# Attention and gated feed-forward on one core: inner rows left in PSUM, softmax sums of four key tiles folded into one, reciprocals laid out 128x9

## The chip, the cores and the metric

The kernel runs on one NeuronCore of a Trainium2 chip. The metric is the device time of one execution in microseconds (us), the median of several runs. The core has a matrix engine (TensorE, PE in the profile; its weight loads are PEld), a vector engine (VectorE, DVE), an activation engine (ScalarE, ACT), a general engine (GpSimd, POOL) and an engine that issues the DMAs (SyncE, SP). Matmul results land in PSUM, 8 banks of 128x512 fp32; everything else lives in SBUF.

## What is computed

8 batches of 8 heads, 576 positions, head size 64. For each head:

```
scores = q k^T / 8 + min(-(cum_i - cum_j), 0)      # cum: running sum of max(s, 0); masked above the diagonal
attn   = exp(scores - rowmax) / (sum + 1e-9)
x      = attn v                                     # heads side by side: 576 x 512 for each batch
h      = max(x w_in, 0)                             # 576 x 1024
c      = cw0 * h[row - 1] + cw1 * h[row] + cw2 * h[row + 1]
out    = (h * sigmoid(c)) w_out                     # 576 x 512 for each batch
```

## The kernel before

**Attention.** Heads go in 32 pairs `p`. Queries lie along the free axis, keys on partitions, in NT = 5 key tiles of 128 (the last has 64 keys). By causality key tile `t` serves only queries from 128t on: widths W_T = 576, 448, 320, 192, 64. For each pair TensorE computes shift scores (`sh_mm`, L1089), of which VectorE takes row maxima (`sh_max`, L1134, which reads PSUM), then the scores proper (`sc_mm`, L1211). ScalarE turns scores into exponentials (`sc_exp`, L1233) in the SBUF tile `pt`, one for each head of the pair, and GpSimd clears what lies above the diagonal (`sc_mask`, L1246, for pairs from B0 = 8 on).

**Sums.** `sums` (L1289) adds the exponentials over the keys by matmuls with a one-hot 128x32 weight. It cuts the 576 queries into 4 pieces of RS = 144, one for each 32-column strip of the array, so that four such matmuls run beside each other. Head 0 goes to strips 0 to 3, head 1 to strips 3 to 0, so each strip of 32 partitions in one bank (`sb_`) holds one piece of each head in its first two rows. All five key tiles are summed: 28 calls a pair, each of which the trace shows as two matmul instructions. `pv_mm` (L1271) then multiplies the exponentials with `v` into the two banks `pv`, of which there is one set.

**The normalization chain** of a pair: `guard` (ScalarE, L1308) copies the sums' bank, 128x144, to `rs`; `inverse` (VectorE, L1313) takes the reciprocal of all 128x144; `store_ri` (DMA, L1318) writes it to DRAM; `spread` (two DMAs, L1327) reads it back, repeated over 64 partitions for each head; `norm` (VectorE, L1335) multiplies `pv` with it and frees `pv`; `x_hi` and `x_lo` (L1350, L1354) split the result into two fp32r parts.

**Feed-forward** (`moe_h`, `moe_o`). A batch needs the x of its four pairs. It is done in two halves of 288 rows and eight inner tiles `f` of 128, taken two at a time (`fp`). For each f: 12 matmuls of 290 columns into one PSUM bank `hb` (`h_mm`, L1386); `relu` (ScalarE, L1397) from the bank to the SBUF tile `ht`, after which the bank is free; `center` (ScalarE L1409 or VectorE L1411) writes cw1 * h to `ct`; two `tap`s (VectorE, L1422) add the neighbours from `ht`. For two f together: `gate` (ScalarE, L1438, 576 wide), `mul` (VectorE, L1444, 576 wide, ct * ht), and a split into two fp32r parts `u` (L1451, L1455). `moe_o` (L1483) multiplies u with w_out, 24 matmuls for each output tile, and `evac` (L1500) moves it out.

**Order.** Every step is a task; a planner written in the kernel (`Sched.play`) simulates the engines with an estimated cost of each task and fixes the order of each engine at build time. What it takes next is set by due times, the table `DUE`, one number for each task in the order of their creation. Buffers are handed out by the planner from pools: 6 PSUM banks (beside the two of `pv`), 3 `pt`, 3 `ht`, 3 `ct`. A task whose option ends in `True` is not planned beside another such task on the other of VectorE and GpSimd. For pairs from B0 on, TensorE's work on pair n's scores, pair n+1's shift scores and pair n-1's `sum` and `pv` is one uninterrupted burst in the order of `ORDER`: sh0, sum, pv, sh1, sc0, sh2, sc1, sc2, sh3, sc3; it starts when all that its members need is there. Each sh and sc step takes two banks. Between bursts TensorE does feed-forward work. The tiles `ht` and `ct` also serve, early on, to prepare the weights.

Of the kernel before, what the change touches and what calls it, by code (L numbers as in the profile page):

```python
# [11 lines left out]
F32 = mybir.dt.float32  # L12
# [18 lines left out]
B1 = 6  # L31
SCRATCH = 1024
# [1566 lines left out]
```

## Time and profile before

| | |
|---|---|
| median of 3 runs | 806.12 us (805.84 to 806.18) |
| profiled execution | 809.6 us |
| its span, first to last instruction | 807.9 us |
| PE busy | 774.9 us, 96% |
| DVE, ACT, POOL busy | 544.8, 439.5, 328.7 us |

The span is that of one profiled execution; its own time is 1.7 us longer than the span and 3.5 us longer than the median of the runs. Busy times are unions of the engine's instructions, so that four matmuls beside each other count once.

### The profile page before, as it was taken

The numbers are of one execution on the slowest core, as the hardware profiler recorded it, in microseconds if no ns is written. First come the engines' busy times: TensorE is split into PE (matmuls) and PEld (weight loads), VectorE is DVE, ScalarE is ACT, GpSimd is POOL, SyncE is SP. The second block draws the span as 40 slices with busy tenths as digits, with TensorE's granted clock in tenths as the row PEclk, the third lists the DMA queues.
The fourth block names the chain that finished last, engine by engine and source line by source line (L and its number), as shares of the span: only waits on it lengthen the run. The fifth ranks groups of instructions, "written<-read, shape, count | busy, mean of one in ns | idle before, by whom it ended". The sixth has DMA issues, their size and how long they took to land.

```text
span 807.9 us, 21422 instructions
## 1 busy us (share of the span) xinstructions
PE 774.9 (96%) x8557; PEld 690.7 (85%) x8557; DVE 544.8 (67%) x1310; ACT 439.5 (54%) x989; POOL 328.7 (41%) x508
## 2 busy tenths in 40 slices
PE   2899899999999999999999999999999999999998
PEld 1566566898999989998998989998898989998998
DVE  7789979747675867766566757667576576825532
ACT  5355446746455646546555646646554555744543
POOL 7122324344534455544435445553435454422122
PEclk9999989999999999999999999999999999999999
DMA  7654354221423232241414233241414221111001
GB/s 241 209 146 150 109 153 145 86 83 46 141 68 124 77 119 96 79 138 53 141 49 132 87 111 105 75 137 57 140 49 125 96 84 43 43 35 42 17 29 37
DMA packets 57369, 78.77 MB, mean 97 GB/s; under 512 B 6521, under 2 KB 39609, under 8 KB 57209
## 3 DMA queue, kind: packets, MB, share of 16 engines
q1 hardware_dynamic: 57269, 77.40, 30.2%
q8 instruction: 67, 1.10, 0.6%
q14 instruction: 33, 0.27, 0.1%
HBM read 63.94 MB, written 13.19 MB: 95 GB/s over the span
## 4 chain that ended last, share of the span: by engine, by line
PE 90%; DVE 4%; ACT 3%; DMA 1%; issue 1%; POOL 0%; SPq 0%; ACTq 0%; DVEq 0%; POOLq 0%
PE ps L1483 26%; PE ps L1386 25%; PE ps L1211 15%; PE pv L1271 11%; PE ps L1289 7%; PE ps L1089 4%; DVE ps L1134 2%; DMA ek<-bx 1%; PE ps L1101 1%; PE ps L1215 1%; ACT pt L1233 1%; PE ps L1095 1%; PE ps L1160 0%; ACT bx L784 0%; DVE ct L880 0%
## 5 line engine op out<-in xcount | busy, mean ns | idle before, releaser
L1483 PE MATMUL ps<-u,wo 128*128 128x288 f32 x1536 | 220.3, 299 | 0.7 <-ACT ob L1500 0.5
L1386 PE MATMUL ps<-x,wi 128*128 128x290 f32 x1536 | 217.5, 298 | 0.3 <-ACT pt L1233 0.2
L1422 DVE SCALAR_TENSOR_TENSOR ct<-ht,cw_sb,ct 128x288 f32<-128x288 f32 (+1 forms) x256 | 154.6, 617 | 84.7 <-ACT ct L1409 81.2
L1483 PEld LDWEIGHTS ps<-u,wo 128*128 128x128 f32 x1536 | 208.3, 188 | 3.6 <-ACT ob L1500 0.7
L1386 PEld LDWEIGHTS ps<-x,wi 128*128 128x128 f32 x1536 | 209.7, 190 | 1.4 <-ACT pt L1233 0.6
L1233 ACT ACTIVATE pt<-ps,bias_sb 128x288 f32<-128x288 f32 (+4 forms) x384 | 154.3, 478 | 88.7 <-PE ps L1211 88.1
L1455 POOL TENSOR_TENSOR u<-ct,u 128x576 fp32r<-128x576 f32 x64 | 94.2, 1477 | 234.2 <-ACT u L1451 201.0
L1134 DVE CUSTOM_DVE_ANT_0 ps<-ps,bb 128x288 f32<-128x288 f32 (+2 forms) x260 | 108.3, 454 | 60.0 <-PE ps L1089 30.6
L1211 PE MATMUL ps<-s 64*128 64x288 f32 (+4 forms) x1152 | 122.8, 309 | 5.7 <-DVE r L1134 4.2
L1066 POOL TENSOR_SCALAR_AFFINE_SELECT bb<-bb 128x256 f32<-128x256 f32 (+1 forms) x130 | 59.4, 466 | 129.5 <-DVE r L1134 102.3
L1211 PEld LDWEIGHTS ps<-s 64*128 64x128 f32 x1152 | 98.3, 190 | 15.7 <-DVE r L1134 10.0
L1025 POOL TENSOR_TENSOR s<-raw,s 128x1152 fp32r<-128x1152 f32 x31 | 83.2, 2684 | 48.1 <-DVE s L1021 36.8
L1271 PE MATMUL pv<-pt,v 128*32 128x448 f32 (+4 forms) x1536 | 96.6, 395 | 1.0 <-DVE rb L1335 1.0
L1397 ACT ACTIVATE ht<-ps 128x289 f32<-128x289 f32 x128 | 52.7, 411 | 80.0 <-PE ps L1386 79.3
L1271 PEld LDWEIGHTS pv<-pt,v 128*32 128x32 f32 x1536 | 60.0, 111 | 33.0 <-issue 26.2
L1246 POOL TENSOR_SCALAR_AFFINE_SELECT pt<-pt 128x128 f32<-128x128 f32 (+1 forms) x240 | 67.7, 302 | 22.0 <-ACT pt L1233 20.4
L1211 PE MATMUL ps<-eq,ek 64*128 64x288 f32 (+4 forms) x384 | 68.5, 323 | 0.0
L1409 ACT ACTIVATE ct<-ht,cw_sb 128x288 f32<-128x288 f32 x121 | 64.9, 536 | 5.4
L1089 PE MATMUL ps<-s 64*128 64x288 f32 (+4 forms) x384 | 61.9, 345 | 3.7 <-DVE r L1134 1.8
L1289 PE MATMUL ps<-pt,onehot 128*32 128x144 f32 (+4 forms) x1792 | 61.4, 273 | 0.2 <-ACT pt L1233 0.2
L1438 ACT ACTIVATE ct<-ct 128x576 f32<-128x576 f32 x64 | 43.5, 680 | 31.4 <-DVE ct L1422 30.6
L1289 PEld LDWEIGHTS ps<-pt,onehot 128*32 128x32 f32 x1792 | 54.8, 113 | 6.5 <-issue 1.1
(90 smaller groups left out, 671.0 us busy)
## 6 DMA issues: line engine op xcount, KB each, us to landing
raw<-qk SPq DMA_DIRECT2D x32, 576.0 KB
bb<-cum_d SPq DMA_DIRECT2D x26, 576.0 KB
v<-vp SPq DMA_DIRECT2D x32, 320.0 KB
rb<-ri_d SPq DMA_DIRECT2D x64, 144.0 KB
outT<-ob SPq DMA_DIRECT2D x64, 144.0 KB
ht<-w_out SPq DMA_DIRECT2D x16, 256.0 KB
w<-w_in SPq DMA_DIRECT2D x8, 512.0 KB
ri_d<-ri SPq DMA_DIRECT2D x32, 72.0 KB
```

Of the source, the lines that this page charges most:

```text
L1025: tt_on(e)(st[:, 0:2, :], R_t[raw.slot], st[:, 2:4, :].bitcast(F32), op=ALU.subtract)
L1089: nc.tensor.matmul(dst[j], l, S_t[sb.slot][r, 2, c0:c1], start=True, stop=not early)
L1134: nc.vector.tensor_tensor_reduce(out=src, in0=src, in1=in1, scale=1.0, scalar=acc if c0 else -3.0e38, op0=ALU.add, op1=ALU.max, accum_out=acc,
L1211: nc.tensor.matmul(dst[j], l, m, start=(k == 0), stop=(k == 3))
L1233: nc.scalar.activation(PT_t[pts[j].slot][0:jt, O_T[t] + c0 : O_T[t] + c1], bank(pb, o, o + c1 - c0)[0:jt], AF.Sigmoid, bias=bias_sb[0:jt, ...
L1246: nc.gpsimd.affine_select(out=reg, in_=reg, pattern=[[1, dg]], compare_op=ALU.is_ge, fill=0.0, base=0, channel_multiplier=-1,)
L1271: nc.tensor.matmul(pvt[gs, o0 : o0 + c1 - c0], vt[0:jt, t, gs], PT_t[pts[g // 2].slot][0:jt, O_T[t] + c0 : O_T[t] + c1], start=(t == 0), s ...
L1289: nc.tensor.matmul(bank(sb_, o0, o0 + b_ - a_)[32 * g : 32 * g + 32], onehot[:, j, :], src[:, a_ - c0 : b_ - c0], start=t == 0 and j == 0, ...
L1386: nc.tensor.matmul(bank(hb, 0, XW), l, r, start=(k == 0), stop=(k == len(seq) - 1))
L1422: nc.vector.scalar_tensor_tensor(cc[:, lo:hi], h_[:, sh + lo : sh + hi], cw_sb[:, 3 * f + k : 3 * f + k + 1], cc[:, lo:hi], op0=ALU.mult, ...
L1455: tt_on(e)(uu[:, 1], C_t[ct.slot], uu[:, 0].bitcast(F32), op=ALU.subtract)
L1483: nc.tensor.matmul(bank(pb, 0, HS), l, r, start=(fp == 0 and k == 0), stop=(fp == NF // 2 - 1 and k == len(seq) - 1),)
```

## The change

1. **Inner rows stay in PSUM.** `relu` writes its result back over the bank `hb`; `center` (now ScalarE only), both `tap`s and `mul` read the bank. The bank is held until `mul`, not until `relu`. `gate` and `mul` are done for each f (288 wide, 128 of each) and no longer for two (576 wide, 64 of each). `ht` is no longer used by the feed-forward, and `tap` and `mul` lose the flag `True`.
2. **Partial sums of the exponentials**, for pairs from D0 = 7 on (25 of 32). For each head a 128x448 tile, taken from the pool `ht`, gets key tile 0 (queries 128 on) + key tile 1, then + tile 2 (320 wide), then + tile 3 (192 wide), by tensor_tensor adds on VectorE or GpSimd. `sums` then multiplies the one-hot weight with the first 128 queries of tile 0, this partial tile, and tile 4: 12 calls a pair for 28. The new adds are waited for by `sum`, and so by the start of the burst.
3. **Reciprocals 128x9.** A new step `gather` (two DMAs) brings the 2 x 4 rows of 144 sums from `rs` into `rc`, 128x9; `inverse` is taken of that; `store_ri` writes 4.6 KB instead of 74 KB; `spread` reads the same bytes from other places.
4. `DUE` has 3780 numbers for 3470, and all of them are new.

```diff
+D0 = 7
 DUE = (
...
-    ri_t = const.tile([P, RS], F32, name="ri")
+    RW = 2 * S // P
+    rc_t, ri_t = (const.tile([P, RW], F32, name=n) for n in ("rc", "ri"))
-    ri_d = dram.tile([P, RS], F32, name="ri_d")
+    ri_d = dram.tile([P, RW], F32, name="ri_d")
...
+        dense = p >= D0
+        acc = [buf("ht"), buf("ht")] if dense else []
+        added = []
+
+        def partial(j):
+            return H_t[acc[j].slot].rearrange("p a c -> p (a c)")[:, 0 : S - P]
+
+        def key_sum(j, t):
+            def run(e):
+                a = partial(j)
+                src = PT_t[pts[j].slot]
+                o = P * (t - 1)
+                (nc.vector if e == "DVE" else nc.gpsimd).tensor_tensor(
+                    a[:, o:], src[:, P : S] if t == 1 else a[:, o:],
+                    src[:, O_T[t] : O_T[t] + W_T[t]], op=ALU.add,
+                )
+            return run
+
+        if dense:
+            for t in range(1, L):
+                for j in range(2):
+                    t_ad = add(
+                        f"ad{p}.{j}.{t}",
+                        [("DVE", c_tt(W_T[t]), True), ("POOL", c_pool(W_T[t]), True, 2.0)],
+                        [m for k, h, m in masks if h == j and (k == t or t == 1 and k == 0)]
+                        + ([added[-2]] if t > 1 else []),
+                        tq - 4, key_sum(j, t), alloc=[acc[j]] if t == 1 else [],
+                        uses=[pts[j]] + ([acc[j]] if t > 1 else []),
+                    )
+                    added.append(t_ad)
+
+        def sums(e):
+            if dense:
+                todo = [(0, 0), (1, 0), (0, 1), (1, 1), (L, 0), (L, 1)]
+            else:
+                todo = [(t, j) for t in range(NT) for j in range(2)]
+            for t, j in todo:
...
+                c1 = P if dense and t == 0 else S
+                if dense and t == 1:
+                    src = partial(j)
...
-        t_sum = add(f"sum{p}", [("PE", 1.5)], [t_ident] + [m for t, m in masks], tq, sums,
-                    alloc=[sb_], uses=pts, mode="c32", burst=group(p + 1))
+        t_sum = add(f"sum{p}", [("PE", 0.62 if dense else 1.5)], [t_ident] + [m for _, _, m in masks] + added,
+                    tq, sums, alloc=[sb_], uses=[*pts, *acc], mode="c32", burst=group(p + 1))
...
+        def gather(e):
+            for j in range(2):
+                nc.sync.dma_start(rc_t[j * D : (j + 1) * D], rs_t[j : 97 + j : 32])
+
+        t_rc = add(f"rc{p}", [("SP", 0.8)], [t_grd], tq, gather, uses=[ri], nbytes=4608)
+
         def inverse(e):
-            nc.vector.reciprocal(ri_t, rs_t)
+            nc.vector.reciprocal(ri_t, rc_t)
...
-                    ri_d.tensor, ri_d.offset + (97 * RS if j else 0),
-                    [(0, D), (-32 * RS if j else 32 * RS, 4), (1, RS)],
+                    ri_d.tensor, ri_d.offset + (7 * RS if j else 0),
+                    [(0, D), (-RS if j else RS, 4), (1, RS)],
...
-            def relu(e, i=i, hb=hb):
-                nc.scalar.activation(
-                    H_t[ht.slot][:, i, 0 : HS + 1], bank(hb, hf, hf + HS + 1), AF.Relu
-                )
+            def relu(e, hb=hb):
+                h = bank(hb, hf, hf + HS + 1)
+                nc.scalar.activation(h, h, AF.Relu)
...
-                    cc[:, lo:hi], h_[:, sh + lo : sh + hi],
+                    cc[:, lo:hi], bank(hb, hf + sh + lo, hf + sh + hi),
...
+            def gate(e, i=i):
+                cc = C_t[ct.slot][:, i, :]
+                nc.scalar.activation(cc, cc, AF.Sigmoid)
+
+            t_g = add(f"ga{b}.{hf}.{f}", [("ACT", c_act(HS))], [t_k], tg + 0.2, gate, uses=[ct])
+
+            def mul(e, i=i, hb=hb):
+                cc = C_t[ct.slot][:, i, :]
+                nc.vector.tensor_tensor(cc, cc, bank(hb, 2 * hf, 2 * hf + HS), op=ALU.mult)
```

## Rows read from the trace of the kernel before

**Rows 1.** The page: busy time of the engines, share of the span, instructions.
```profile
PE 774.9 (96%) x8557; PEld 690.7 (85%) x8557; DVE 544.8 (67%) x1310; ACT 439.5 (54%) x989; POOL 328.7 (41%) x508
```

**Rows 2.** Busy time by stretches: start:end, length, busy us of each engine (instructions), clock, DMA.
```profile
0.00:100.00 100.00, 78.32 (x848) 52.43 (x848) 82.42 (x192) 47.23 (x103) 35.13 (x47) 0.98 0.55 169
100.00:740.00 640.00, 632.26 (x7240) 574.71 (x7237) 436.55 (x1074) 362.80 (x829) 280.47 (x453) 0.99 0.29 93
740.00:808.00 68.00, 64.28 (x475) 63.57 (x473) 25.88 (x46) 29.48 (x59) 13.07 (x9) 1.00 0.10 34
```

**Rows 3.** One burst on PE in order of time: start, us, instructions, [idle before].
```profile
418.61 0.40 PE L1089 MATMUL ps<-s 64*128 64x288 f32 x2
418.94 1.77 PE L1289 MATMUL ps<-pt,onehot 128*32 128x144 f32 x54
...
424.93 0.67 PE L1211 MATMUL ps<-s 64*128 64x288 f32 x6 [0.39 <-DVE r L1134]
...
428.18 2.66 PE L1483 MATMUL ps<-u,wo 128*128 128x288 f32 x18
...
436.83 1.77 PE L1289 MATMUL ps<-pt,onehot 128*32 128x144 f32 x54
```

**Rows 4.** Busy time in that burst: its sums, its pv, its scores.
```profile
418.94:420.49 1.55, 1.55 (x56) 1.53 (x56) 1.55 (x5) 1.46 (x4) 0.00 (x0) 1.00 0.00 0
420.49:423.39 2.90, 2.90 (x59) 1.92 (x51) 1.78 (x4) 1.28 (x3) 2.42 (x2) 1.00 0.10 27
423.39:428.18 4.79, 4.41 (x61) 4.04 (x58) 4.03 (x17) 3.01 (x8) 2.71 (x8) 1.00 0.46 133
```

**Rows 5.** DVE groups, page and by shape: count, busy us, mean ns, idle before.
```profile
L1422 DVE SCALAR_TENSOR_TENSOR ct<-ht,cw_sb,ct 128x288 f32<-128x288 f32 (+1 forms) x256 | 154.6, 617 | 84.7 <-ACT ct L1409 81.2
...
L1444 DVE TENSOR_TENSOR ct<-ct,ht 128x576 f32<-128x576 f32 x64 | 48.3, 756 | 15.2 <-ACT ct L1438 14.5
...
L1313 DVE RECIPROCAL ri<-rs 128x144 f32<-128x144 f32 x32 | 33.6, 1049 | 12.8 <-ACT rs L1308 12.3
...
L1134 DVE CUSTOM_DVE_ANT_0 ps<-ps,bb,r 128x288 f32<-128x288 f32 x52 | 25.1, 522 | 26.4 <-PE ps L1089 26.4
...
L1134 DVE CUSTOM_DVE_ANT_0 ps<-ps,bb 128x288 f32<-128x288 f32 x52 | 23.1, 470 | 25.0 <-PE ps L1089 22.4 <-ACT ht L1397 2.6
...
L760 DVE TENSOR_SCALAR ncr<-pt 64x9 f32<-64x9 f32 x1 | 0.2, 231 | 0.0
```

**Rows 6.** Lines L1422 and L1354 on DVE: ns min/median/max.
```profile
L1422 DVE SCALAR_TENSOR_TENSOR ct<-ht,cw_sb,ct x256: 500/518/2455, 132.3 to 793.5; 128x287 f32<-128x287 f32 x64, 128x288 f32<-128x288 f32 x64
...
L1354 DVE TENSOR_TENSOR x<-rb,x x27: 748/960/3110, 61.0 to 747.2; 128x580 fp32r<-128x580 f32 x27
```

**Rows 7.** The same burst on SP, on DVE and on POOL, in order of time.
```profile
422.30 0.33 SPq L1318 DMA_DIRECT2D ri_d<-ri  x1
...
424.00 1.27 SPq L1327 DMA_DIRECT2D rb<-ri_d  x2
...
426.73 0.52 DVE L1422 SCALAR_TENSOR_TENSOR ct<-ht,cw_sb,ct 128x287 f32<-128x287 f32 x1
...
430.30 0.75 DVE L1335 TENSOR_TENSOR rb<-pv,rb 128x576 f32<-128x576 f32 x1
432.09 2.03 DVE L1354 TENSOR_TENSOR x<-rb,x 128x580 fp32r<-128x580 f32 x1 [1.03 <-ACT x L1350]
436.96 0.47 DVE L1134 CUSTOM_DVE_ANT_0 ps<-ps,bb 128x288 f32<-128x288 f32 x1 [2.84 <-PE ps L1089]
...
430.07 0.79 POOL L1246 TENSOR_SCALAR_AFFINE_SELECT pt<-pt 128x128 f32<-128x128 f32 x3 [0.15 <-ACT pt L1233]
```

**Rows 8.** The first 100 us: one norm on DVE, and the pv that follows on PE.
```profile
92.86 0.75 DVE L1335 TENSOR_TENSOR rb<-pv,rb 128x576 f32<-128x576 f32 x1
...
93.66 4.60 PE L1271 MATMUL pv<-pt,v 128*32 128x128 f32 x48 [0.99 <-DVE rb L1335]
```

**Rows 9.** ACT after the last h ahead of that burst: its center.
```profile
419.22 0.54 ACT L1409 ACTIVATE ct<-ht,cw_sb 128x288 f32<-128x288 f32 x1
```

More of the change, by code (lines that the diff above doesn't have):

```diff
@@ L1253, in pair @@
                                     A + 0.1 * i, sc_mask, uses=[pts[j]])
-                    masks.append((t, t_exp))
+                    masks.append((t, j, t_exp))
                     o += w
@@ L1277, in pv_mm @@
             return run
-        def sums(e):
-            for t in range(NT):
-                for j in range(2):
-                    src = PT_t[pts[j].slot][:, O_T[t] : O_T[t] + W_T[t]]
-                    c0 = P * t
-                    for q in range(c0 // RS, 4):
-                        g = 3 - q if j else q
-                        a_, b_ = max(c0, q * RS), (q + 1) * RS
-                        o0 = a_ - q * RS
-                        nc.tensor.matmul(
-                            bank(sb_, o0, o0 + b_ - a_)[32 * g : 32 * g + 32], onehot[:, j, :],
-                            src[:, a_ - c0 : b_ - c0], start=t == 0 and j == 0,
-                            stop=t == NT - 1, tile_position=(0, 32 * g),
-                            skip_group_check=True,
-                        )
@@ L1296, in pair @@
         ta = A1 + 1
         tq = ta - TQA
-        t_sum = add(f"sum{p}", [("PE", 1.5)], [t_ident] + [m for t, m in masks], tq, sums,
-                    alloc=[sb_], uses=pts, mode="c32", burst=group(p + 1))
-        t_pv = add(f"pv{p}", [("PE", 2.82)], [t_v] + [m for t, m in masks], tq + 0.1,
+        dense = p >= D0
[3 more added lines that the diff above has]
+            return H_t[acc[j].slot].rearrange("p a c -> p (a c)")[:, 0 : S - P]
@@ new lines, in sums @@
+        def sums(e):
[4 more added lines that the diff above has]
+            for t, j in todo:
+                src = PT_t[pts[j].slot][:, O_T[t] : O_T[t] + W_T[t]]
+                c0 = P * t
+                c1 = P if dense and t == 0 else S
+                if dense and t == 1:
+                    src = partial(j)
+                for q in range(c0 // RS, 4):
+                    g = 3 - q if j else q
+                    a_, b_ = max(c0, q * RS), min(c1, (q + 1) * RS)
+                    if a_ >= b_:
+                        continue
+                    o0 = a_ - q * RS
+                    nc.tensor.matmul(
+                        bank(sb_, o0, o0 + b_ - a_)[32 * g : 32 * g + 32], onehot[:, j, :],
+                        src[:, a_ - c0 : b_ - c0], start=j == 0 and (t == 0 or dense and t == 1 and q > 0),
+                        stop=t == NT - 1, tile_position=(0, 32 * g), skip_group_check=True,
+                    )
@@ L1301, in pair @@
+        t_sum = add(f"sum{p}", [("PE", 0.62 if dense else 1.5)], [t_ident] + [m for _, _, m in masks] + added,
+                    tq, sums, alloc=[sb_], uses=[*pts, *acc], mode="c32", burst=group(p + 1))
+        t_pv = add(f"pv{p}", [("PE", 2.82)], [t_v] + [m for _, _, m in masks], tq + 0.1,
                    pv_mm(range(NT)), alloc=[pv], uses=[vb, *pts], mode="c32",
                    prev=None if p + 1 >= B0 else t_sum, burst=group(p + 1))
-        note(p + 1, "sum", t_sum, [t_v] + [m for t, m in masks])
+        note(p + 1, "sum", t_sum, [t_v] + [m for _, _, m in masks] + added)
@@ L1310, in pair @@
         t_grd = add(f"gd{p}", [("ACT", c_act(RS))], [t_sum], tq, guard, alloc=[ri], uses=[sb_])
+        def gather(e):
+            for j in range(2):
+                nc.sync.dma_start(rc_t[j * D : (j + 1) * D], rs_t[j : 97 + j : 32])
+        t_rc = add(f"rc{p}", [("SP", 0.8)], [t_grd], tq, gather, uses=[ri], nbytes=4608)
         def inverse(e):
-            nc.vector.reciprocal(ri_t, rs_t)
-        t_inv = add(f"inv{p}", [("DVE", 1.06)], [t_grd], tq, inverse, uses=[ri])
+            nc.vector.reciprocal(ri_t, rc_t)
+        t_inv = add(f"inv{p}", [("DVE", 0.15)], [t_rc], tq, inverse, uses=[ri])
         def store_ri(e):
             nc.sync.dma_start(ri_d, ri_t)
-        t_ri = add(f"ri{p}", [("SP", 0.34)], [t_inv], tq, store_ri, uses=[ri], nbytes=73728)
+        t_ri = add(f"ri{p}", [("SP", 0.34)], [t_inv], tq, store_ri, uses=[ri], nbytes=4608)
         def spread(e):
@@ L1370, in moe_h @@
     def moe_h(b, hf, fp):
-        u, ht, ct = buf("u"), buf("ht"), buf("ct")
-        tg = h_tag(b, hf, 2 * fp)
-        taps, t_mm = [], None
+        u, ct = buf("u"), buf("ct")
+        products, t_mm = [], None
         for i in range(2):
@@ L1390, in moe_h, with center, tap @@
             xs = [x_bufs[b * HP + c][hf] for c in range(NC)]
+            tg = h_tag(b, hf, f)
             t_mm = add(f"h{b}.{hf}.{f}", [("PE", 1.61)],
                        [x_done[b * HP + c] for c in range(NC)] + [t_wi[f]],
-                       h_tag(b, hf, f), h_mm, alloc=[hb] + ([u, ht, ct] if i == 0 else []),
+                       tg, h_mm, alloc=[hb] + ([u, ct] if i == 0 else []),
                        uses=xs, prev=t_mm if i else None)
-            def relu(e, i=i, hb=hb):
+            def relu(e, hb=hb):
+                h = bank(hb, hf, hf + HS + 1)
+                nc.scalar.activation(h, h, AF.Relu)
+            t_relu = add(f"re{b}.{hf}.{f}", [("ACT", 0.41)], [t_mm], tg, relu, uses=[hb])
+            def center(e, i=i, f=f, hb=hb):
                 nc.scalar.activation(
-                    H_t[ht.slot][:, i, 0 : HS + 1], bank(hb, hf, hf + HS + 1), AF.Relu
-                )
-            t_relu = add(f"re{b}.{hf}.{f}", [("ACT", 0.41)], [t_mm], h_tag(b, hf, f), relu,
-                         uses=[hb, ht])
-            def center(e, i=i, f=f):
-                o = C_t[ct.slot][:, i, :]
-                src = H_t[ht.slot][:, i, hf : hf + HS]
-                w = cw_sb[:, 3 * f + 1 : 3 * f + 2]
-                if e == "ACT":
-                    nc.scalar.activation(o, src, AF.Copy, scale=w)
-                else:
-                    nc.vector.tensor_scalar(o, src, w, None, op0=ALU.mult)
-            t_c = add(f"ce{b}.{hf}.{f}", [("ACT", 0.53), ("DVE", 0.36, True, 2.0)],
-                      [t_relu, t_cw], h_tag(b, hf, f) + 0.1, center, uses=[ht, ct])
-            def tap(e, k, i=i, f=f):
-                h_ = H_t[ht.slot][:, i, :]
+                    C_t[ct.slot][:, i, :], bank(hb, 2 * hf, 2 * hf + HS), AF.Copy,
+                    scale=cw_sb[:, 3 * f + 1 : 3 * f + 2],
+                )
+            t_k = add(f"ce{b}.{hf}.{f}", [("ACT", 0.53)], [t_relu, t_cw], tg + 0.1, center,
+                      uses=[hb, ct])
+            def tap(e, k, i=i, f=f, hb=hb):
                 cc = C_t[ct.slot][:, i, :]
@@ L1426, in tap @@
                 )
-            t_k = t_c
             for k in (0, 2):
-                t_k = add(f"ta{b}.{hf}.{f}.{k}", [("DVE", 0.53, True)], [t_k],
-                          h_tag(b, hf, f) + 0.1, lambda e, k=k, tap=tap: tap(e, k), uses=[ht, ct])
-            taps.append(t_k)
-        tg = h_tag(b, hf, 2 * fp + 1) + 0.2
-        def gate(e):
-            cc = C_t[ct.slot]
-            nc.scalar.activation(cc, cc, AF.Sigmoid)
-        t_g = add(f"ga{b}.{hf}.{fp}", [("ACT", c_act(2 * HS))], taps, tg, gate, uses=[ct])
-        def mul(e):
-            cc = C_t[ct.slot]
-            nc.vector.tensor_tensor(
-                cc, cc, H_t[ht.slot][:, :, hf : hf + HS], op=ALU.mult
-            )
-        t_m = add(f"mu{b}.{hf}.{fp}", [("DVE", c_tt(2 * HS), True)], [t_g], tg, mul, uses=[ct, ht])
+                t_k = add(f"ta{b}.{hf}.{f}.{k}", [("DVE", 0.53)], [t_k], tg + 0.1,
+                          lambda e, k=k, tap=tap: tap(e, k), uses=[hb, ct])
+            def gate(e, i=i):
[5 more added lines that the diff above has]
+                nc.vector.tensor_tensor(cc, cc, bank(hb, 2 * hf, 2 * hf + HS), op=ALU.mult)
+            products.append(add(f"mu{b}.{hf}.{f}", [("DVE", c_tt(HS))], [t_g], tg + 0.2, mul,
+                                uses=[hb, ct]))
+        tg = h_tag(b, hf, 2 * fp + 1) + 0.2
         def u_hi(e):
```

2 lines of the change are left out of this document (1 added, 1 removed), and 475 rows, old and new, of the table DUE.

## The prediction

> **What bounds the kernel now.** I read the page first, then stretches, then one burst in order of time. The page says that PE is busy for 774.9 of 807.9 us, 96%, and no other engine over 67% [rows 1]. The stretches say where the rest lies, and that the clock is granted at 0.98 to 1.00 throughout [rows 2]: 21.7 us idle in the first 100 us (loading, set-up), 7.7 us in the 640 us from 100 to 740, and 3.7 us in the tail of feed-forward work. So from 100 us on a microsecond taken from PE is a microsecond of the kernel, as long as what PE waits for does not become later. In the burst at 418.6 [rows 3] the reader is to see that PE passes through shift scores, sums, pv and scores to the o matmuls at 428.18 with a gap of 0.39 us, for a row maximum of DVE (4.41 of the last 4.79 us are busy). The sums hold it for 1.55 us, pv for 2.90 us, the rest of the scores for 4.79 us [rows 4].
>
> **The sums on PE.** Before, a strip of the array takes 800 columns of sums a pair (160 + 640 or 320 + 480, both heads), pv 1600. Per strip column that is 1.55/800 = 1.94 ns, and 2.90/1600 = 1.81 ns for pv [rows 4]. After, the columns are 128 + 448 + 64 a head: the strips get 352, 288, 288 and 352. At 1.94 ns a column 352 columns take 0.68 us; by the count, 24 instructions for 56 at 1.55/56 = 27.7 ns, it is 0.66. Lower bound, at pv's price: 0.64. Upper bound: the diagonal 128 columns and the last 64 go to one strip each, and if nothing ran beside them the time would be 2 x (128 + 160 + 64) x 1.81 ns = 1.27 us (160 is the busiest strip's part of the 448). Strips did run beside each other before, or 800 columns would not fit in 1.55 us, so I take 0.69 and a gain of 0.86 us a pair: 25 x 0.86 = **21.5 us** (bounds 7 and 23). The first 7 pairs keep their sums. The wait for partial tiles is priced below; the feed-forward's and pv's matmuls do not change.
>
> **DVE and ACT.** The work here is beside PE, so it costs nothing while it stays in time. Reciprocal: 32 x 1049 ns go; 9 elements should take some 0.23 us, as the 64x9 operation does [rows 5], so -26 us. Adds: 150 of 448, 320 and 192 columns. The 576-wide tensor_tensor at 756 ns [rows 5] less the columns missing at 1.04 ns gives 0.62, 0.49 and 0.36 us, 2.9 us a pair, +73 us if DVE does all, and less of it if GpSimd takes some. Multiplications: 128 at 470 ns for 64 at 756 [rows 5] (470 is the 288-wide operation of one PSUM and one SBUF operand), +12 us. The taps: their median is 518 ns but their mean is 617 (155 us for 256 [rows 5]), with a longest of 2.46 us [rows 6]. The nearest operation with a PSUM operand and a per-partition scalar, the row maximum of 288 columns, takes 522 ns on the mean [rows 5]. So I take the taps at 520 ns, -25 us; between no change and that lies the bound. DVE goes from 545 to some 580 us (605 without the taps' gain), 72 to 77% of the span. ACT gets 128 gates 288 wide for 64 twice as wide; at no more than the 0.54 us of a center of that width [rows 9] that adds under 64 x 0.54 = 35 us to 440. Neither becomes the bound.
>
> [...]
> [...]
>
> **The chain of the normalization.** In the burst above the reciprocal's store is issued at 422.30 and the reading back at 424.00, so a small DMA lands within 1.7 us; norm runs at 430.30 to 431.05 and the next sums begin at 436.83, pv 1.55 us later [rows 3, 7]. The gather adds two issues of 0.33 us (SP's price of such a store) and 1.7 us of landing, and takes 0.8 us off the reciprocal: the chain is some 1.6 us longer, against 7 us of slack. So nothing from 100 us on. Behind the reciprocal in DVE's queue stand row maxima, so if the gather lands late they are late, and with them PSUM banks; that is in the bounds. In the first 100 us there is no slack in one place: pv at 93.66 waited 0.99 us for the norm that ended at 93.61 [rows 8]. There 7 pairs get a chain 1.6 us longer; the worst case is all of it each time, 11 us, the best nothing. I take **+2 us**, that of one or two pairs, since only one pv shows such a wait.
>
> **Banks and adds before a burst.** A bank of h is now held through center, two taps, gate and mul. Relu and center of the last h ahead of the burst end at 419.76 [rows 9], and its second tap at 427.25 [rows 7], inside the burst; with the old order the bank would be held past that. After pv the burst takes 14 bank fillings in 4.79 us. Six banks give each 2.05 us. Center, two taps, gate (at center's price) and mul need 0.54 + 1.04 + 0.54 + 0.47, some 2.6 us, and sums and pv after the change still give 3.6 us before the banks are wanted. So it fits if the engines take this work at once, and the new order of tasks can put o matmuls, which end with one copy, last before a burst. The last masks of this burst ended at 430.86, the second half of the partial sums needs four adds, 1.7 us, and DVE is held until 434.12 by a subtraction that took 2.03 us [rows 7], where 0.75 is its best [rows 6]. The next burst's sums start at 436.83, the burst itself 0.33 us before them, as the one before it does [rows 3]: the adds fit with 0.7 us to spare. PE idles 7.7 us from 100 to 740 now [rows 2]; I add a quarter for these handoffs, **+2 us** (bounds: none, and the rivals below).
>
> **The sum.** -21.5 + 2 + 2 = -17.5 us. On the profiled execution that is 809.6 to 792.1 us; its time is 3.5 us over the median of the runs, so in the runs' terms 806.1 to **788.5 us**.
>
> **Rivals.**
> *h holds a bank in the bursts* (the slower side). If one of six banks is held through the scores of a burst, the same 14 fillings find five banks: 4.79 x 6/5 = 5.75 us, 0.96 us more, and over 24 bursts 23 us: 788.5 + 23 = 812 us. For it: the taps of [rows 7] that ran inside the burst, and that PE's one gap there is a wait for a bank's row maximum. Against it: the due times are all new, and sums and pv leave 3.6 us. It decides from 0.73 us a burst (17.5/24).
> *Adds late.* The gap between bursts from 428.2 to 436.5 [rows 3] is short; if half the gaps are, and DVE or GpSimd bring the last adds 1 us late in those 12, PE stands or takes work out of turn: +12 us, 800 us. For it: the 0.7 us to spare; against: GpSimd can take adds, and between 434.12 and 436.96 DVE had nothing to do [rows 7].
> *The sums don't shorten.* If the 12 calls run strip after strip (1.27 us), the gain is 7 us, and with the two charges above the time is 803 us; if the handoffs cost the rest, 806 us. Against: 56 instructions in 1.55 us now.
> *More than the sums.* Taps out of GpSimd's way shorten waits, DVE's maxima come sooner, head and handoffs cost nothing, and half of the 7.7 us idle goes: 806 - 21.5 - 4 = 780 us, and with sums at 0.64 us 0.05 x 25 less, 779.
>
> **How the numbers follow.** Forecast as summed, 783 to 795: 0.58. More than the sums, about 779: 0.12. Adds late or part of the bank wait, about 800: 0.14. Sums not shorter, 803 to 806: 0.05. A bank held in every burst, about 812: 0.11. For a range of 8 in 10 I leave out the last of these and a tail at the other end: 777 to 804. A measurement of this kernel tells about 0.2%, 1.6 us, from no change. Faster by more: the first three cases and half of the fourth, 0.86; the same: 0.04; slower: the bank case less what of it lands near zero, 0.10.
>
> **What would show it.** Right: L1289 shows 24 instructions a pair from the eighth pair on and about 0.7 us from the first sum to pv; PE busy falls to about 754 us with idle time unchanged within 5 us; the taps' mean is near 520 ns; reciprocals near 0.2 us; pv waits for norm only in the first 110 us. Wrong: PE waits inside the bursts for DVE's mul, or before them for adds; a sum that takes over 1 us; DVE over 640 us busy; reciprocals that stand in DVE's queue for the gather. The prediction falls if the idle time of PE from 100 to 740 grows by more than 10 us.

## The result, and the profile after

The changed kernel takes 780.41 us (median of 4 runs, 778.85 to 781.13), the kernel before, run beside it, 806.15 (805.84 to 806.22): the ratio is 0.968 with an interval of 0.966 to 0.970, a gain of 25.7 us. Forecast were 788.5 us and a range of 777 to 804; the time lies in the range, and the gain is half as large again as the 17.5 us of the sum. The profiled execution took 780.03 us.

The page after, in the line that answers to [rows 1]:
```profile
PE 739.3 (95%) x7757; PEld 662.2 (85%) x7757; DVE 518.1 (67%) x1443; ACT 454.6 (58%) x1069; POOL 389.6 (50%) x573
```
PE is still the bound: it is busy for 35.6 us less, in a span 29.8 us shorter. The stretches that answer to [rows 2], cut where the same stages end (columns as there):
```profile
0.00:100.00 100.00, 76.68 (x866) 53.44 (x868) 83.32 (x205) 46.86 (x105) 31.47 (x42) 0.95 0.59 176
100.00:712.00 612.00, 600.52 (x6432) 547.11 (x6429) 410.93 (x1188) 378.55 (x898) 343.95 (x522) 1.00 0.31 93
712.00:778.00 66.00, 62.14 (x465) 61.67 (x464) 23.84 (x53) 29.23 (x67) 14.18 (x10) 1.00 0.08 28
```
Length less PE's busy time is its idle time: 23.3 us in the head, 11.5 in the middle, 3.9 in the tail, for 21.7, 7.7 and 3.7 before [rows 2]. So some of what the sums gave is handed back in the middle. The burst that answers to [rows 3], on PE in order of time:
```profile
399.36 0.40 PE L1112 MATMUL ps<-s 64*128 64x288 f32 x2
399.69 0.30 PE L1353 MATMUL ps<-pt,onehot 128*32 128x128 f32 x1
399.70 0.32 PE L1353 MATMUL ps<-ht,onehot 128*32 128x144 f32 x3
...
400.28 0.30 PE L1294 MATMUL pv<-pt,v 128*32 128x128 f32 x2
...
403.17 0.40 PE L1112 MATMUL ps<-s 64*128 64x288 f32 x2
```
From the first sum at 399.69 to the first pv at 400.28 it is 0.59 us, where before it was 1.55 [rows 4]; pv takes 2.89 us as it did. From the eighth pair on each of the 25 pairs shows 0.59 or 0.60. The vector engine's groups, which answer to [rows 5]:
```profile
L1484 DVE SCALAR_TENSOR_TENSOR ct<-ps,cw_sb,ct 128x287 f32<-128x287 f32 (+1 forms) x256 | 131.2, 514 | 83.3 <-ACT ct L1471 79.0 <-PE ps L1453 1.6
L1502 DVE TENSOR_TENSOR ct<-ct,ps 128x288 f32<-128x288 f32 x128 | 57.4, 448 | 20.2 <-ACT ct L1496 19.5
L1317 DVE TENSOR_TENSOR ht<-ht,pt 128x320 f32<-128x320 f32 (+1 forms) x75 | 52.3, 725 | 7.9 <-POOL pt L1269 7.1 <-POOL ht L1317 0.6
L1317 DVE TENSOR_TENSOR ht<-pt 128x448 f32<-128x448 f32 x19 | 15.6, 821 | 5.8 <-POOL pt L1269 5.8
...
L1380 DVE RECIPROCAL ri<-rc 128x9 f32<-128x9 f32 x32 | 6.7, 210 | 3.8 <-DMA rc<-rs 3.8
```
Taps (L1484) lost 23.4 us and reciprocals (L1380) 26.9; multiplications (L1502) cost 9.1 more, and the adds (L1317) brought 67.9 us for 94 of the 150, GpSimd taking 56. The split L1354, now L1422, went over to GpSimd in 12 cases. DVE as a whole is 27 us less busy.

**Where the middle handed back.** Between the sums of pair 9 and those of pair 28 both kernels do the same feed-forward work (876 matmuls of h, 912 of o, read from the lines) and 19 pairs' sums. That stretch in the kernel before:
```profile
235.15:663.54 428.39, 424.06 (x4925) 390.86 (x4923) 289.78 (x729) 244.16 (x554) 204.57 (x344) 1.00 0.31 99
```
and after:
```profile
223.70:637.59 413.89, 405.44 (x4317) 372.26 (x4315) 281.42 (x810) 256.05 (x603) 250.82 (x393) 1.00 0.32 100
```
PE's work fell by 18.6 us, that is 0.98 a pair, and the stretch by 14.5: idle time rose from 4.3 to 8.5 us. The waits of PE from 100 to 712 us in the kernel after name what is new (total us, times, longest):
```profile
PE ps L1234 <- DVE r L1157: 4.9, 13, 0.5
PE ps L1353 <- DVE ob L1559: 1.9, 1, 1.9
PE ps L1453 <- ACT ob L1559: 1.2, 1, 1.2
PE ps L1112 <- ACT ob L1559: 0.9, 1, 0.9
```
The scores' waits for row maxima cost 4.9 us where they cost 4.2 before from 100 to 712 (and one shift score waited 1.2 us for such a maximum there); new are three single waits, 4.0 us together, for the copy `evac` that empties a bank of output. The first of them, on DVE in order of time:
```profile
325.63 4.40 DVE L1317 TENSOR_TENSOR ht<-ht,pt 128x320 f32<-128x320 f32 x4 [1.31 <-POOL pt L1269]
329.95 0.74 DVE L1403 TENSOR_TENSOR rb<-pv,rb 128x576 f32<-128x576 f32 x1
330.62 0.44 DVE L1559 COPY ob<-ps 128x288 f32<-128x288 f32 x1
```
and on GpSimd at that time:
```profile
326.08 2.66 POOL L1048 TENSOR_TENSOR s<-raw,s 128x1152 fp32r<-128x1152 f32 x1
```
Four adds take 4.40 us while GpSimd works on two SBUF tiles; the shortest add takes 0.34 us. Behind them stand the norm and the copy, and the sums of that burst wait 1.90 us for the bank. The other two waits look alike: at 412.15 two adds of 192 columns take 3.30 us beside a GpSimd operation of 2.66, at 589.34 four take 4.20 beside one of 3.04, and the copy that PE waits for then stands behind the norm, on ACT behind the cast that waits for the norm.

### The profile page after: what moved, and what is told of

It is laid out like the page before. It is cut to its first block, busy times and chain, and to the rows that moved or that the text cites. A ratio compares the mean times of both kernels' runs of the same rounds, so it can differ in the third digit from the quotient of the medians.

```text
span 778.1 us, 20353 instructions
## 1 busy us (share of the span) xinstructions
PE 739.3 (95%) x7757; PEld 662.2 (85%) x7757; DVE 518.1 (67%) x1443; ACT 454.6 (58%) x1069; POOL 389.6 (50%) x573
## 4 chain that ended last, share of the span: by engine, by line
PE 85%; DVE 4%; issue 2%; ACT 2%; POOL 1%; DMA 0%; SPq 0%; DVEq 0%; ACTq 0%; POOLq 0%
PE ps L1453 26%; PE ps L1542 25%; PE ps L1234 13%; PE pv L1294 10%; PE ps L1353 4%; PE ps L1112 4%; DVE ps L1157 1%; ACT pt L1256 1%; DVE ht L1317 1%; PE ps L1238 1%; PE ps L1124 1%; POOL u L1514 1%; DVE r L1157 1%; PE ps L1183 1%; PE ps L1118 0%
## 5 line engine op out<-in xcount | busy, mean ns | idle before, releaser
L1256 ACT ACTIVATE pt<-ps,bias_sb 128x288 f32<-128x288 f32 (+4 forms) x384 | 155.8, 478 | 82.2 <-PE ps L1234 81.8
L1484 DVE SCALAR_TENSOR_TENSOR ct<-ps,cw_sb,ct 128x287 f32<-128x287 f32 (+1 forms) x256 | 131.2, 514 | 83.3 <-ACT ct L1471 79.0
L1234 PE MATMUL ps<-s 64*128 64x288 f32 (+4 forms) x1152 | 119.6, 307 | 6.4 <-DVE r L1157 4.9
L1234 PEld LDWEIGHTS ps<-s 64*128 64x128 f32 x1152 | 95.3, 188 | 15.7 <-DVE r L1157 11.2
L1089 POOL TENSOR_SCALAR_AFFINE_SELECT bb<-bb 128x256 f32<-128x256 f32 (+1 forms) x130 | 55.3, 433 | 82.0 <-DVE r L1157 43.4
L1466 ACT ACTIVATE ps<-ps 128x289 f32<-128x289 f32 x128 | 50.8, 397 | 73.9 <-PE ps L1453 70.5
L1269 POOL TENSOR_SCALAR_AFFINE_SELECT pt<-pt 128x128 f32<-128x128 f32 (+1 forms) x240 | 72.6, 322 | 13.5 <-ACT pt L1256 12.9
L1496 ACT ACTIVATE ct<-ct 128x288 f32<-128x288 f32 x128 | 56.3, 439 | 33.2 <-DVE ct L1484 32.6
L1502 DVE TENSOR_TENSOR ct<-ct,ps 128x288 f32<-128x288 f32 x128 | 57.4, 448 | 20.2 <-ACT ct L1496 19.5
L1471 ACT ACTIVATE ct<-ps,cw_sb 128x288 f32<-128x288 f32 x128 | 63.9, 499 | 5.1
L1112 PE MATMUL ps<-s 64*128 64x288 f32 (+4 forms) x384 | 59.7, 343 | 3.8 <-DVE s L1044 1.2
L1317 DVE TENSOR_TENSOR ht<-ht,pt 128x320 f32<-128x320 f32 (+1 forms) x75 | 52.3, 725 | 7.9 <-POOL pt L1269 7.1
```

The source lines that it names most:

```text
L1112: nc.tensor.matmul(dst[j], l, S_t[sb.slot][r, 2, c0:c1], start=True, stop=not early)
L1234: nc.tensor.matmul(dst[j], l, m, start=(k == 0), stop=(k == 3))
L1256: nc.scalar.activation(PT_t[pts[j].slot][0:jt, O_T[t] + c0 : O_T[t] + c1], bank(pb, o, o + c1 - c0)[0:jt], AF.Sigmoid, bias=bias_sb[0:jt, ...
L1269: nc.gpsimd.affine_select(out=reg, in_=reg, pattern=[[1, dg]], compare_op=ALU.is_ge, fill=0.0, base=0, channel_multiplier=-1,)
L1471: nc.scalar.activation(C_t[ct.slot][:, i, :], bank(hb, 2 * hf, 2 * hf + HS), AF.Copy, scale=cw_sb[:, 3 * f + 1 : 3 * f + 2],)
L1484: nc.vector.scalar_tensor_tensor(cc[:, lo:hi], bank(hb, hf + sh + lo, hf + sh + hi), cw_sb[:, 3 * f + k : 3 * f + k + 1], cc[:, lo:hi], op ...
```

## Experiments

Times are medians, and a ratio is to the kernel before as run beside that kernel. It took 806.15 us beside the kernels of the first three experiments and of the long reciprocal, 809.42 beside the short sums alone, the two with exchanged due times and the partial sums in the first seven pairs, and 805.27 beside the other four. A lead or a loss inside a kernel is read at the start of the copies `guard`, one for each pair, in two traces. The mean granted clock of PE in the profiled execution is 0.993 in the kernels before and after. It is lower in six of the runs below: 0.977 with the inner rows in SBUF, 0.985 and 0.982 with the gather right ahead of the reciprocal, 0.983 and 0.948 with exchanged due times, 0.951 with partial sums in all pairs. What is missing to 1, times the span, bounds what PE lost by it after its first rise: 5.4 us in the kernel after, 19 with the rows in SBUF, 47 at 0.948.

**All 28 calls, the adds kept.**
```diff
-            if dense:
-                todo = [(0, 0), (1, 0), (0, 1), (1, 1), (L, 0), (L, 1)]
-            else:
-                todo = [(t, j) for t in range(NT) for j in range(2)]
+            todo = [(t, j) for t in range(NT) for j in range(2)]
...
-                if dense and t == 1:
-                    src = partial(j)
...
```


> The changed kernel with its order of tasks, but the sums of every pair are done in all 28 calls; the partial sums are still added up and then not used. Theory (from 100 us on the kernel's time is PE's time, and a sum went from 1.55 to 0.59 us in 25 pairs): all of 25 x 0.96 = 24 us comes back, 804 us (802 to 807). Rival (the gain lies mostly in the new order, the head or the feed-forward's rows, and PE has room in the bursts): 781 to 793 us.

806.91 us, ratio 1.001 (0.999 to 1.004). Pair 7's sums, and pair 31's, on PE:
```profile
179.13 1.77 PE L1348 MATMUL ps<-pt,onehot 128*32 128x144 f32 x54
...
716.73 1.77 PE L1348 MATMUL ps<-pt,onehot 128*32 128x144 f32 x54
```
In the kernel after they start at 180.14 and 693.38. This kernel goes from 1.0 us ahead to 23.4 behind, 24.4 us over 24 pairs' sums: 1.02 us a pair. With the 28 calls back nothing of the gain is left. The lead at pair 7 is still there, but between the sums of pairs 9 and 28 this kernel takes 433.5 us where the kernel before takes 428.4.

**The adds left out, their place in the order kept.** The sums read key tile 1 in place of the partial tile.
```diff
         def key_sum(j, t):
             def run(e):
-                a = partial(j)
...
+                pass
...
-                if dense and t == 1:
-                    src = partial(j)
```


> The changed kernel without the 150 adds: the sums are done in 12 calls, but read key tile 1 in place of the partial tile, so tiles 2, 3 and part of 0 are left out of the sums. Theory (the adds lie beside PE): 780 us, within 2 us. Rival (the adds make bursts start late or hold up DVE's row maxima, which is where 3.5 us of the sums' gain went between the tenth and the 29th pair): 776 us or less, and PE's idle time from 100 to 712 us falls from 11.5 to 8 us or less.

777.60 us, ratio 0.965 (0.960 to 0.969), beside 0.968 (0.966 to 0.970) of the kernel after: the times do not tell the two apart. The traces do: this one is 4.4 us behind the kernel after at pairs 7 to 9 (from the head, below) and 0.4 at pair 28, so it wins 3.9 us in the stretch where 4.1 us of idle time were new, and the three waits for `evac` are not among its waits. The adds cost those 4 us; no further cost shows.

**The inner rows in SBUF again, all else as after.**
```diff
-                h = bank(hb, hf, hf + HS + 1)
-                nc.scalar.activation(h, h, AF.Relu)
+                nc.scalar.activation(rows(i, hf, hf + HS + 1), bank(hb, hf, hf + HS + 1), AF.Relu)
...
-                    cc[:, lo:hi], bank(hb, hf + sh + lo, hf + sh + hi),
+                    cc[:, lo:hi], rows(i, hf + sh + lo, hf + sh + hi).bitcast(F32),
...
```


> The changed kernel with its order of tasks, but relu writes the inner rows to SBUF (into room of the tile u that is not used until later, rounded to fp32r), and center, taps and multiplication read them there. Theory (feed-forward work on DVE has room beside PE): the taps' mean rises from 514 ns to 570 to 640, DVE is busy 15 to 35 us longer, and the time stays at 780 us within 2 us. Rival (faster taps and fewer clashes with GpSimd gave several us): 784 to 790 us.

823.25 us, ratio 1.021 (1.018 to 1.024): 43 us over the kernel after, and slower than before. That part 1 lies beside PE and is worth nothing there is refuted for this order of tasks. Its taps and multiplications by groups:
```profile
L1487 DVE SCALAR_TENSOR_TENSOR ct<-u,cw_sb,ct 128x287 f32<-128x287 f32 (+1 forms) x256 | 180.5, 712 | 69.3 <-ACT ct L1474 66.9
L1505 DVE TENSOR_TENSOR ct<-ct,u 128x288 f32<-128x288 f32 x128 | 73.0, 570 | 20.7 <-ACT ct L1499 18.7
```
DVE is busy for 577.8 of 820.7 us, 70%, and yet PE waits 14.7 us in place of 4.9 for row maxima, and for copies and u besides. Of the 42.6 us between the two spans, 22.8 are idle time of PE (61.6 for 38.8) and 19.8 a longer busy time on the same matmuls (759.1 for 739.3). Most of the second part is the clock, here from 100 us on and around one of its falls:
```profile
100.00:752.00 652.00, 619.56 (x6433) 560.48 (x6434) 464.99 (x1187) 382.88 (x897) 353.50 (x522) 0.98 0.29 88
337.00:345.00 8.00, 7.96 (x53) 7.57 (x54) 3.79 (x19) 5.11 (x12) 6.24 (x13) 0.57 0.19 48
```
The kernel after has 1.00 in its middle; 0.02 of 652 us is some 13 us. The clock falls five times in this stretch, to the lower of the two levels that the column shows (in the kernel after it reads 0.50 from 72 to 81 us and 1.00 from 82 to 700), and each fall begins in a wait of PE of 1.57 to 3.74 us, or within 0.5 us of its end.

**The same, with one operand of every tap in PSUM.** The multiplication reads the bank too.
```diff
-                    cw_sb[:, 3 * f + k : 3 * f + k + 1], cc[:, lo:hi],
+                    cw_sb[:, 3 * f + k : 3 * f + k + 1], bank(hb, hf + sh + lo, hf + sh + hi),
...
```


> The changed kernel with its order of tasks; relu writes the rows to SBUF, center reads them there, and each tap multiplies them and adds the bank in PSUM in place of what center left (so the sum over the three rows is left out); the multiplication reads the bank. No tap has two SBUF inputs now. Theory (rows in SBUF cost 43 us because taps and multiplications with two SBUF inputs were held up by GpSimd, up to 4.7 us one of them): taps at 515 to 530 ns on the mean, 780 us within 3 us. Rival (it is the SBUF tile itself, its waits or ScalarE's write to SBUF): 800 us or more.

780.61 us, ratio 0.966 (0.962 to 0.970), and its guards are all within 0.6 us of those of the kernel after. The tap line, min/median/max in ns, of the run with the rows in SBUF:
```profile
L1487 DVE SCALAR_TENSOR_TENSOR ct<-u,cw_sb,ct x256: 501/518/4737, 120.1 to 807.6; 128x287 f32<-128x287 f32 x64, 128x288 f32<-128x288 f32 x64
```
and of this one:
```profile
L1487 DVE SCALAR_TENSOR_TENSOR ct<-u,cw_sb,ps x256: 500/514/519, 120.5 to 765.0; 128x287 f32<-128x287 f32 x64, 128x288 f32<-128x288 f32 x64
```
Relu's and center's other room in SBUF costs nothing; the 43 us come with the operations that have two SBUF operands, PE's waits and the lower clock behind them included; the longest tap goes from 4737 to 519 ns. With the rows in SBUF 58 of the 62 taps over 650 ns run beside a tensor_tensor of GpSimd, and 23 of the other 194; here 106 of the 256 do, and none takes over 519 ns. The traces of the two kernels agree: before, where the taps read both operands from SBUF, 30 of the 32 taps over 650 ns run beside such an operation and 19 of the other 224; after, with one operand in PSUM, 108 of the 256 do, and none takes over 521 ns.

**The long reciprocal, no gather, in the order after.**
```diff
-                nc.sync.dma_start(rc_t[j * D : (j + 1) * D], rs_t[j : 97 + j : 32])
+            pass
...
-            nc.vector.reciprocal(ri_t, rc_t)
+            nc.vector.reciprocal(ri_t, rs_t)
...
```


> The changed kernel with its order of tasks, but without the gather: the reciprocal is taken of 128x144 and stored whole, as before. Theory (the chain of the normalization and DVE's time have room): reciprocals at 1050 ns again, DVE busy 27 us longer, the time at 780 us within 2 us. Rival 1 (DVE's 27 us sit in front of row maxima that PE waits for): 784 us or more. Rival 2 (the gather's landing held DVE's queue up): 778 us or less.

796.86 us, ratio 0.990 (0.986 to 0.994), 16.5 us over the kernel after. Where the reciprocal stands on DVE, first in the kernel after:
```profile
404.58 0.21 DVE L1380 RECIPROCAL ri<-rc 128x9 f32<-128x9 f32 x1
404.71 0.21 DVE L1157 CUSTOM_DVE_ANT_0 ps<-ps,bb 128x64 f32<-128x64 f32 x1
```
and here:
```profile
416.01 1.05 DVE L1379 RECIPROCAL ri<-rs 128x144 f32<-128x144 f32 x1
416.98 0.21 DVE L1157 CUSTOM_DVE_ANT_0 ps<-ps,bb 128x64 f32<-128x64 f32 x1
```
It is issued between row maxima of the burst, and the next of them starts 0.13 us after it in the one and 0.97 in the other. PE's waits for row maxima go from 4.9 us (13) to 9.6 (27), and the guards fall behind by 10.8 us from pair 7 to pair 31, 0.45 a pair. PE's idle time grew by 3.1 of these 10.8 us; 6.4 are a longer busy time on the same matmuls of scores and shift scores, which the list of waits does not show, and why they take longer is not told. No pv waits for a norm. Before pair 7 it loses 2.1 us; 4.1 us it was late at pair 0 already, in the way told in the last section.

**The short reciprocal in the order before, gather issued right ahead of it,** alone:
```diff
         def inverse(e):
-            nc.vector.reciprocal(ri_t, rs_t)
+            for j in range(2):
+                nc.sync.dma_start(rc_t[j * D : (j + 1) * D], rs_t[j : 97 + j : 32])
+            nc.vector.reciprocal(ri_t, rc_t)
...
```


> The kernel before with its order of tasks and its sums in 28 calls, and only the reciprocals laid out 128x9, with the gather issued right ahead of the reciprocal. Theory (under sums and pv of 4.45 us the long reciprocal was hidden, so nothing is gained; the chain has 7 us of slack): 804 to 808 us. Rival 1 (shorter DVE work pays by itself, as its absence cost 16 us in the new order): 800 us or less. Rival 2 (the longer chain costs in the head): 810 us or more.

and with the short sums of the experiment after this one:

> The kernel before with its order of tasks, the sums of pairs 7 to 31 in 12 calls (key tile 1 read in place of a partial tile, nothing added up), and the reciprocals laid out 128x9, with the gather issued right ahead of the reciprocal. Short sums alone came to 0.974 of before, 785 us, 3 us short of the 24 us that they save PE. Theory (with sums shortened, the 1.05 us reciprocal no longer fits into DVE's time under sums and pv, and holds up row maxima; 0.21 us fits): the rest comes back, 779 to 783 us. Rival (the gather's landing, some 2 us, is waited for by DVE and costs as much as the reciprocal did): 785 us or more.

823.17 us, ratio 1.019 (1.015 to 1.024), and 810.11 us, 1.005 (1.002 to 1.009). The wait of DVE for the gather, in the first:
```profile
DVE ri L1316 <- DMA rc<-rs: 82.2, 31, 6.1
```
and in the second:
```profile
DVE ri L1322 <- DMA rc<-rs: 69.3, 32, 5.1
```
DVE stands 82.2/31 = 2.7 and 69.3/32 = 2.2 us a pair for the landing, with row maxima behind it, and PE waits 11.8 and 16.8 us for these. In the kernel after, the order puts other work into that time: DVE waits twice, 3.8 us in all.

**Short sums alone, in the order before.** The 12 calls from pair 7 on, with key tile 1 in the place of the partial sums.
```diff
+            dense = p >= 7
+            if dense:
+                todo = [(0, 0), (1, 0), (0, 1), (1, 1), (L, 0), (L, 1)]
...
```


> The kernel before with its order of tasks and one edit: the sums of pairs 7 to 31 are done in 12 calls, with key tile 1 read in place of a partial tile (tiles 2, 3 and part of 0 are left out of the sums, nothing is added up). Theory (PE-bound, 0.96 us a pair): 806.2 - 24 = 782 us (780 to 785). What is over from 782 to 780.4 is then the net of all else in the change. Rival (the old order does not let PE go on earlier, other engines come due): 788 us or more.

788.41 us, ratio 0.974 (0.969 to 0.979); to the 806 us beside most other runs it is a gain of 18 us. From pair 7 to pair 31 the guards gain 16.4 us, 0.68 a pair of the 0.96: PE's waits for row maxima rise from 4.2 us to 7.1. The sums' gain is there without any other part, and some 70% of it stays under an order made for longer sums.

**The due times exchanged.** The kernel after with the due times of the kernel before (an add gets those of a mask or an exponential of its tile, a gather those of the reciprocal):
```diff
 DUE = (
-    -132125, -2922, -2421, -1663, -1776, -2831, -5701, -5544, -1538, -1779, -20212, -18757,
...
```


> The changed kernel with the due times of the kernel before: each task that both have keeps its old number, gate and multiplication of each f take that of their pair of f, an add that of the mask (or exponential) it follows, the gather that of the reciprocal. Theory 1 (banks of h now held until the multiplication need an order made for it; the old order runs into bursts with banks held): 790 us or more, with PE waiting inside bursts or standing idle between tasks. Theory 2 (the order is of no account, the sums are all): 780 to 784 us.

816.22 us, ratio 1.011 (1.007 to 1.014). The kernel before with the due times of the kernel after, where the two f of a pair take the second's:
```diff
 DUE = (
-    -71591, -3748, -2936, -3146, -2870, -3586, -4314, -2902, -3422, -2825, -6319, -11723, -11558,
...
```


> The kernel before with the due times of the changed one (gate and multiplication of a pair of f take those of its second f). If the new due times by themselves saved the time in the head (10 us of lead at the eighth pair in the two traces, of which 0.9 us is a sum): 797 to 803 us. If they are only fit for the changed tasks: 806 us or more.

909.69 us, ratio 1.125 (1.117 to 1.132). Each table fits its own kernel: 36 us are lost in the one, 100 in the other, up to 41 of the 100 by the lower clock. So the gain is not in the due times by themselves, and the three other parts do not bring it without them.

**Partial sums in the first seven pairs too.** The new adds get the due time of their tile's exponential.
```diff
-D0 = 7
+D0 = 0
...
```


> The changed kernel with partial sums in all 32 pairs (D0 = 0); the adds of the first seven pairs get the due times of the exponentials that they follow. Theory (PE is the bound in the head too, 95% busy from 40 to 100 us): 780.4 - 7 x 0.96 = 773.7 us, less what the head's waits take, 774 to 777 us. Rival (in the head the normalization chain, DVE and the weights' use of the tiles ht set the pace): 780 us or more.

840.24 us, ratio 1.040 (1.034 to 1.045). PE's first wait, by total:
```profile
PE ps L1360 <- DVE ht L1324: 26.1, 4, 23.6
```
One add comes 23.6 us late in the first 100 us; by pair 6 the kernel is 61 us behind and stays there. The tiles `ht` prepare the weights at that time, and these due times were made for D0 = 7; which of the two makes it so late is not told apart.

**Short sums in the first seven pairs, no adds there.** Key tile 1 stands for the partial sums in those pairs.
```diff
-            if dense:
+            short = True
+            if short:
                 todo = [(0, 0), (1, 0), (0, 1), (1, 1), (L, 0), (L, 1)]
...
```


> The changed kernel with its order of tasks, but the sums of the first seven pairs too are done in 12 calls, with key tile 1 read in place of a partial tile in those seven (no adds there). Theory (PE sets the pace in the head too): 7 x 0.96 = 6.7 us less, 773 to 775 us. Rival (the head waits for the normalization chain and DMAs): within 2 us of 780 us.

778.09 us, ratio 0.964 (0.959 to 0.970). At pair 6 it is 4.3 us ahead of the kernel after, where 7 x 0.96 would be 6.7; from pair 15 on 2.6 are left. So PE sets the head's time in part: at most some 60% of what its sums lose is gained there, as the clock was 0.97 over the first 100 us for 0.95 in the kernel after, worth up to 2 us. What is lost again stands in one place, between pairs 14 and 15: behind a wait of 1.9 us that the kernel after has too, the clock fell here (0.72 from 326 to 332 us) and not there, and 46 matmuls of pv behind it take 4.53 us for 2.87.

## Why the prediction was right, and by how much not

The time lies in the range of 777 to 804, but the case that was forecast (783 to 795, chance 0.58) did not occur.

**What bounds the kernel** held: PE does, and in the order after a microsecond off its sums is one off the kernel, as 1.02 us a pair come back with the 28 calls. PE's busy time on sums fell from 61.45 to 35.77 us, 25.7; 24.2 of it in the 25 shortened pairs, the rest in sums of the first seven pairs, of which two took 3.33 us in place of 1.83 in the profiled execution of the kernel before, and one in that of the kernel after. That it equals the difference of the medians is chance, since the head and the middle add terms of their own. PE's whole busy time fell to 739.3 us and not to the 754 forecast: 10 us of it lie before pair 7.

**The sums on PE** were mis-sized, by 2.6 us: 0.59 us a pair in place of 0.69, so 25 x 0.965 = 24.1 us for 21.5. I scaled the price of a strip column in the old sums (1.94 ns) and took pv's for a lower bound; 0.59 over 352 columns is 1.68 ns, under both, and 0.59 over 24 instructions is 24.6 ns, under the 27.7 of the count. The upper case, strip after strip (1.27 us), is out: the 0.59 us hold the 128 and 64 columns that go to single strips as well.

**The head** was mis-signed: +2 us forecast, and no pv waits for a norm any more. But that is not where the gain lies. Pair 7's sums, before which no sums are shortened, start at 189.22 us before and at 180.14 after. Some 4 of these 9.1 us belong to the profiled execution of the kernel before, not to the change (last section): the run with the short sums alone, the same program up to there, starts them at 185.02. The medians then hold a gain of some 5 us. Of it 2.1 come with the short reciprocal: the run with the long one loses that from pair 0 to pair 7. The other 3 us are open. Up to pair 7's sums PE does the same matmuls in these runs and idles as long (24.2 us before, 24.8 with short sums alone, 25.0 after), so the gain is in its busy time (165.1, 160.2 and 155.1 us), not in shorter waits; the order of the head is new, and no run put it back by itself.

**Banks and adds**: +2 us forecast, 3.8 measured in PE's idle time of the middle, under the bound of 10 that I had named. No bank of h is waited for in the order after, so the rival that prices it at 812 us did not occur; the due times of before, at 816, show that an order can cost that much, but not that it is this bank. The rival of late adds was right in kind and too large: three late copies behind held-up adds, 4.0 us, not 12. An add was priced at 0.36 to 0.62 us; the adds took 0.34 at best and 3.46 at worst, and the norm and the copy that stood behind the late ones were not in the prediction.

So in place of -21.5 + 2 + 2 the runs say -24.1 - 5 + 3.4 = -25.7; the 3.4 is what remains of the 29.8 us between the spans after 9.1 of the head and 24.1 of the sums. The time is that of the rival "more than the sums" (779 to 780), and of its reasons the head that costs nothing and the cheaper sum held, though the head for another reason than the waits. The taps did come out of GpSimd's way (none takes over 521 ns, where the longest took 2455 before [rows 6]), but the scores' waits for row maxima did not shorten with them (4.9 us for 4.2 from 100 to 712); the last reason, half of the idle time, went the other way.

**DVE and ACT.** The terms were near: taps 514 ns for 520, reciprocals 210 for 230, multiplications 448 for 470, ACT 15 us more for a bound of 35. The taps do go to their best time with a PSUM operand, and are not dearer: 514 against a median of 518 [rows 6]. DVE's total fell to 518 where I had 580, but not by adds that went to GpSimd: the 94 that stayed took 67.9 us of the 73 priced for all 150. The 1.04 ns a column of that price is what the row maxima show before (647, 514 and 381 ns for 448, 320 and 192 columns), and the shortest adds of these widths took 614, 478 and 343 ns; but 24 of the 94 took over 0.3 us more than the shortest of their width, 22.5 us in all, 21 of them beside a tensor_tensor of GpSimd, where 15 of the other 70 ran. Most of the rest of the difference is work that the new order put on other engines: splits (27 on DVE before, 15 after) and casts of queries and keys (22 before, 9 after). Refuted is the sentence that this work "is beside PE, so it costs nothing while it stays in time" as I used it. At 68 to 70% busy, DVE made the kernel some 13 of the 16.5 us slower with 0.84 us a pair in front of row maxima, and 43 us with taps and multiplications held up beside GpSimd (712 and 570 ns on the mean for 514 and 448) and the lower clock that came with PE's waits (0.98 for 1.00 in the middle). So parts 1 and 3, to which I gave no gain, cannot be taken out of this order without losing much of its gain. That they would be needed in any order is not shown: no run has an order of its own made for the sums alone, and in the order of before the sums alone already gave 788.

## What to carry to other kernels

An engine's share of busy time does not say what its work costs: look at what stands in its queue ahead of the operation that frees the bound engine's banks, since 0.84 us there cost 0.45 us a pair at 68% busy. Look at the granted clock as well: with the rows in SBUF five waits of PE of 1.57 to 3.74 us went with stretches at half the clock, some 13 of the 43 us lost, though a wait of 1.90 us in the kernel after did not. Where an order is fixed at build time, a change of durations and a new order belong together: the changed kernel in the old order and the old kernel in the new order were both slower here than neither, while the short sums alone gained in the old order. Matmuls on separate strips of the array took 1.68 to 1.94 ns here for each column of the busiest strip, and what an elementwise operation cost beside GpSimd went by whether one of its operands was in PSUM: the longest tap took 519 ns with one there, and 4737 with both in SBUF.

## What was not expected of the hardware

**When the first matmuls come to full speed differs between executions.** The first sums of the kernel before, on PE in its profiled execution, and its transpose and pv after them:
```profile
43.06 3.33 PE L1289 MATMUL ps<-pt,onehot 128*32 128x144 f32 x56
46.32 0.33 PE L1160 MATMUL ps<-ident,r 128*128 128x128 f32 x1
46.58 2.90 PE L1271 MATMUL pv<-pt,v 128*32 128x128 f32 x48
```
and of the kernel after, the same 28 calls:
```profile
42.99 1.77 PE L1353 MATMUL ps<-pt,onehot 128*32 128x144 f32 x54
```
With the last two of the 56 instructions the 1.77 us are 1.83, so the first sums took 1.8 times as long before. Sums take 3.33 us at the lower level of the clock too: pair 4's before, at 111.09, and pair 2's after, at 77.11, where the column of the granted clock reads 0.50. At 43 us it reads 1.00 in both, and yet matmuls run that slowly until 46.3 us in the one and until about 37 in the other. From 20 to 34 us PE had been busy for 11.3 us in the one and for 9.4 in the other; but in the run with the short sums alone, the same program as before up to there, it was busy for 11.5, and its matmuls are at the shorter times from 35 us on (two of 64 columns take 0.23 us at 35.24, for 0.29 at 35.40 in that of before). So the later rise belongs to the execution and not to the program. Against the kernel after, the run without adds and the one with the long reciprocal are 4.1 us late at pair 0, the three others with the same pair 0 are 0.3 to 0.7 early; the three runs of the kernel before with short sums or the short reciprocal, with its own due times, are 4.3 to 4.7 us earlier there than its profiled execution. So some 4 us between single executions mean nothing, and they are likely most of the 3.5 us by which that execution lies over the median.

**The issue and landing of a 4.6 KB gather** from SBUF to SBUF hold DVE for 2.2 to 2.7 us on the mean when nothing is put before it, more than the reciprocal of 144 columns that it saves (1049 ns [rows 5]).
